# An adaLN block with multi-query attention: a lead in another order, and one scale on another engine

## The chip, the cores and the metric

The kernel runs on one core of a Trainium2 chip. A core has five engines that run their own instruction queues in order: TensorE (PE in the profile; its weight loads are PEld), VectorE (DVE), ScalarE (ACT), GpSimd (POOL) and SyncE (SP, which here only issues DMAs). An instruction starts when the one before it on its engine has been issued and every semaphore that it needs is set. The metric is the device time of one execution in microseconds.

## The reference

The inputs are one batch of S = 2048 rows of width D = 512, one conditioning vector c, and weights. There are H = 32 query heads of size 16 that share one K head and one V head, and F = 1792.

```python
mod = (_silu(c) @ w_mod).reshape(c.shape[0], 6, 1, -1)
sa, ca, ga, sb, cb, gb = (mod[:, 0], mod[:, 1], mod[:, 2], mod[:, 3], mod[:, 4], mod[:, 5])
h = _layernorm(x, axis=-1) * (1 + ca) + sa
x = x + ga * _A_ref(h, A_wq, A_wk, A_wv, A_wo)      # softmax attention, 32 heads, one K and one V
h = _layernorm(x, axis=-1) * (1 + cb) + sb
x = x + gb * _B_ref(h, B_w_gate, B_w_up, B_w_down)  # ((h Wg) * (h Wu)) Wd
```

## The kernel before

The rows are cut into 4 blocks of 512. A unit is one block of queries with 4 of the 32 heads, so there are 32 units; a block's x lies in two groups of 256 rows (`xts[2b]` and `xts[2b+1]`, of two tiles each). Matmuls that need precision run as two f16 halves, high and low, so an operand such as h or wq is first split: a high half, and the rest as a low half.

Softmax subtracts a row maximum. It is computed ahead by the max pass: for each unit PE multiplies q by all keys (L569), DVE reduces each 128x512 result (L573), and the maxima are put into the q tile `sst[u]` as two more rows. While a unit's scores, exponentials and PV products run (`attend`, L620, L622, L631), the max pass of the next unit runs between them. Side work (q projections of later units, weight preparation, the output projection and the gated FFN, all at L484 on PE) fills the gaps.

Before the first unit can attend, everything up to its maxima has to be there. That is the lead. A straight part first loads x, w_mod and wq, computes the modulation, the norm of block 0 and its h, and the first K and q projections. A loop of 30 steps follows (`LEAD`), which for each step n emits, in this order: what was posted before, the max pass, the relus left over, `first[n]`, some matmuls of the first q projection of block 0 (`Q_BURSTS`, steps 26 to 29), and one of the pieces that compute the rest of the modulation (from step 23 on). The max pass does two of its own steps in lead steps 0, 2, ... 12, none in the odd ones up to 13, and one in each from 14 to 29. The first unit has 24 of them: 16 with two plain reduces each (L573; the first 8 over the keys of block 0, the other 8 over block 1), and for blocks 2 and 3 a "diff" matmul pair (keys of block 3 minus those of block 2, for which `kng` holds the negated keys of block 2) whose relu ACT takes (L576) and a combined add and maximum on DVE (L578), 16 in all. The second unit's start at lead step 24.

The dictionary `first` is the order that is written out by hand. Engines are in-order and the schedule is manual, so an entry's place fixes where its instructions stand in each engine's queue. The entries are:

- `ln_stats(i)`: bn_stats and bn_aggr of group i on DVE (L238, L240). `ln_rstd(b)`: the reciprocal deviation of block b on POOL, eight small instructions (L200 to L205, L312, L313). `ln_norm(b, ...)`: four tiles normalised, here two on DVE and two on ACT (L251, L249).
- `ln_tr(b)`: per 128 columns four PE transposes into one PSUM bank (L257) and an ACT evacuation to `hf(b, k)` with the modulation (L260).
- `k_part(b)`, `q_part(u, p)`: eight PE matmuls (L267) and an ACT copy (L269). `combine(key, sel)`: one f32 matmul (two passes, L274) that adds the partial sums and lays out the rows. `k_evac(b)`, `q_evac(u, p)`: the f16 halves of K or q, a high half on ACT (L288) and the rest on DVE (L289). Unit u has two q tiles p = 0, 1; both first units are projected in the lead from block 0's h.
- `v_mm(b)`: eight small PE matmuls (L302), and an ACT copy (L305) posted for the next step.
- `h_halves(b, ks)`: the halves of h of block b on POOL. For block 0 the tile is first scaled in place by `fwd[:, 0:1]` (L422), so a q projection from block 0's unscaled h has to stand ahead of it. Then L424 and L425.
- `wq_squares(ks)`: squares with row sums on ACT (L402). `wq_sum`: their sum over partitions on PE, a DVE reduce, and a power and a scale on POOL (L406 to L410). `wq_scales`: a DVE reciprocal (L413) and two small POOL instructions. `wq_halves(ks)`: the high half on ACT (L420), a scale and the low half on POOL (L422, L425).
- `last_rows()`: the load of the other half of w_mod (3 MB) into the space of x's blocks 0 to 2 (L439). `ev_scales`: constants for the output.

PSUM has eight banks of 128x512 f32, handed out in turn from a queue (`ps_hold`, `ps_give`, `ps_mx`, `ps_sc`): a matmul that is given a bank waits until the one that used it before has been read. `posts` are closures emitted at the start of the next step.

Two pieces of the straight part matter as well: the scales for K, q and h that are computed from four maxima (L359 to L373), and what follows them, in the order `combine(0)`, `combine((0, 0))`, `ln_norm(1)` on DVE, `k_evac(0)`, `q_evac(0, 0)`, `q_part(0, 1)`, `ln_norm(1)` on ACT, `ln_stats(4)`, `ln_stats(5)`, `ln_rstd(2)`.

Of the kernel before, what the change touches and what calls it, by code (L numbers as in the profile page):

```python
# [54 lines left out]
def adaln_mqa_glu_kernel(ctx: ExitStack, tc: tile.TileContext, x_in, wq_in, wk_in, wv_in, wo_in,  # L55
# [175 lines left out]
    def ln_stats(i):  # L231
        if i % 2 == 0:
            stats[i // 2] = (work.tile([128, 4, 2], F32, name="st"), work.tile([128, 4], F32, name="ry0"),
                             work.tile([128, 8], F32, name="nb0"))
        st = stats[i // 2][0]
        bs = [work.tile([128, 6], F32, name="bs", bufs=4) for _ in range(2)]
        for t in range(2):
            nc.vector.bn_stats(bs[t], xts[i][t])  # L238
        for t in range(2):
            nc.vector.bn_aggr(st[:, 2 * (i % 2) + t, :], bs[t])  # L240

    def ln_norm(b, engines):
        st, y, nb = stats[b]
        for j, eng in enumerate(engines):
            if eng is None:
                continue
            xt = xts[2 * b + j // 2][j % 2]
            if eng is nc.scalar:
                nc.scalar.activation(xt, xt, AF.Identity, bias=nb[:, 4 + j:5 + j], scale=y[:, j:j + 1])  # L249
            else:  # L250
                eng.tensor_scalar(xt, xt, st[:, j, 0:1], y[:, j:j + 1], op0=OP.subtract, op1=OP.mult)  # L251
# [20 lines left out]
    def combine(key, sel):  # L272
        p = pks[key] = ps_hold("pk")
        nc.tensor.matmul(p, sel.rearrange("p a r -> p (a r)"), parts[key], start=True, stop=True)  # L274

    def k_part(b):
        partial(b, wkv, b)

    def q_part(u, p):
        partial((u, p), wqs[:, :, 64 * u + 32 * p:64 * u + 32 * p + 32], 0)  # L280

    def q_evac(u, p):
        split_rows(sst[u][:, p, :], pks[u, p], qsc, sck[:, 3:4], 0.0)
        ps_give(pks[u, p])
# [6 lines left out]
    def k_evac(b):  # L291
        cs = slice(b * BT, (b + 1) * BT)
        sc = sckb if b else sck
        split_rows(kst[:, cs], pks[b], sc[:, 0:1], sc[:, 2:3], rows[:, 2:3])
        if b == NB - 2:
            nc.gpsimd.tensor_scalar(kng, kst[:, cs], -1.0, 0.0, op0=OP.mult, op1=OP.add)
        ps_give(pks[b])

    def v_mm(b):
        p = ps_hold("pvt", (128, 4, 16))  # L300
        for i in range(4):
            nc.tensor.matmul(p[:, i, :], parts[b][:, i * 128:(i + 1) * 128], lane[:, 16:32], start=True, stop=True)  # L302

        def out():
            nc.scalar.activation(vst[:, 4 * b:4 * b + 4, 0:16], p, AF.Copy, scale=inv[:, 0:1] if b else 1.0)  # L305
            ps_give(p)
        posts.append(out)

    def ln_rstd(b):
        st, y, nb = stats[b]  # L310
        rstd_into(y, st[:, :, 1], 4)
        nc.gpsimd.tensor_tensor(nb[:, 0:4], st[:, :, 0], y, op=OP.mult)  # L312
        nc.gpsimd.tensor_scalar(nb[:, 4:8], nb[:, 0:4], -1.0, 0.0, op0=OP.mult, op1=OP.add)  # L313
# [53 lines left out]
    qsc = sck[:, 1:2]  # L367
    nc.vector.reciprocal(sck[:, 0:1], kb[:, 6:7])
    nc.vector.tensor_tensor(sck[:, 2:3], rows[:, 0:1], sck[:, 0:1], op=OP.mult)
    nc.gpsimd.tensor_scalar(inv[:, 0:1], kb[:, 4:5], 22.64 * 1.001 * 2.0 ** -15, 2.0 ** -45, op0=OP.mult, op1=OP.max)  # L370
    nc.vector.reciprocal(fwd[:, 0:1], inv[:, 0:1])
    nc.vector.tensor_scalar(hsb, modT[0][:, :, 0:64:32], fwd[:, 0:1], None, op0=OP.mult)
    nc.gpsimd.tensor_scalar(sckb, sck, inv[:, 0:1], 0.0, op0=OP.mult, op1=OP.add)  # L373
    combine(0, selk)
    combine((0, 0), selq)
    ln_norm(1, (nc.vector, None, nc.vector, None))
    k_evac(0)
    q_evac(0, 0)
    q_part(0, 1)
# [57 lines left out]
    def last_rows():  # L437
        wmb = big.tile([128, KC, 1536], F32, name="wmB", tag="wu")
        nc.sync.dma_start(wmb, wm_v[:, :, 1536:3072])  # L439
        wmB.append(wmb)  # L440

    wmB = []
    KA, KB = (0, 1), (2, 3)
    ln_stats(4)
    ln_stats(5)
    ln_rstd(2)
    SA, VE = nc.scalar, nc.vector
    first = {0: lambda: (combine((0, 1), selq), ln_tr(1)),
             1: lambda: (q_evac(0, 1), v_mm(0), ln_stats(6)),
             2: lambda: (k_part(1), ln_norm(2, (VE, SA, VE, SA)), ln_stats(7), ln_rstd(3)),  # L450
             3: lambda: combine(1, selk), 4: lambda: (k_evac(1), ln_tr(2)),
             5: lambda: (last_rows(), ln_norm(3, (VE, SA, VE, SA))),
             6: lambda: (k_part(2), v_mm(1)), 7: lambda: combine(2, selk),
             8: lambda: (k_evac(2), ln_tr(3)), 9: lambda: (q_part(1, 0), v_mm(2)),
             10: lambda: (k_part(3), combine((1, 0), selq), h_halves(3, KA)),
             11: lambda: (q_evac(1, 0), combine(3, selk)), 12: lambda: (k_evac(3), h_halves(3, KB), q_part(1, 1), wq_squares(KA)),
             13: lambda: (v_mm(3), combine((1, 1), selq), wq_squares(KB)), 14: lambda: (q_evac(1, 1), wq_sum()),
             15: lambda: h_halves(0, KA), 16: wq_scales, 17: lambda: h_halves(0, KB), 19: lambda: wq_halves(KA), 20: ev_scales, 21: lambda: wq_halves(KB),
             23: lambda: h_halves(1, KA), 24: lambda: h_halves(1, KB)}
    later_h = deque((2, k) for k in range(KC))  # L460

    TERMS = ((0, 0), (1, 0), (0, 1))
# [816 lines left out]
```

## Time and profile before

| | |
|---|---|
| median of 3 runs | 1686.23 us (1686.07 to 1686.28) |
| profiled execution | 1688.73 us |
| its span, first to last instruction | 1686.7 us |
| mean granted TensorE clock | 0.997 |
| PE busy | 1661.1 us, 98% |
| DVE busy | 1389.7 us, 82% |
| ACT busy | 1217.1 us, 72% |
| POOL busy | 517.2 us, 31% |
| first scores of attention (L620) | 80.56 us from the span's start |

The profile is of one execution under the hardware profiler, so its own time stands beside its span. An engine's busy time is a sum over the whole span and hides stages: PE is busy 98% because it carries attention and the FFN for 1600 us, while the lead is its first 80 us. Where the prediction shows rows in order of time, a row gives start, length, engine, line and operation, the tile written and those read, how many instructions were merged into the row, and in brackets the idle time of the engine just before and what ended it. Matmul lengths include the pipeline, so the distance between starts tells more of a matmul's cost than its length.

### The profile page before, as it was taken

The numbers are of one execution on the slowest core, as the hardware profiler recorded it, in microseconds if no ns is written. First come the engines' busy times: TensorE is split into PE (matmuls) and PEld (weight loads), VectorE is DVE, ScalarE is ACT, GpSimd is POOL, SyncE is SP. The second block draws the span as 40 slices with busy tenths as digits, with TensorE's granted clock in tenths as the row PEclk, the third lists the DMA queues.
The fourth block names the chain that finished last, engine by engine and source line by source line (L and its number), as shares of the span: only waits on it lengthen the run. The fifth ranks groups of instructions, "written<-read, shape, count | busy, mean of one in ns | idle before, by whom it ended". The sixth has DMA issues, their size and how long they took to land.

```text
span 1686.7 us, 33353 instructions
## 1 busy us (share of the span) xinstructions
PE 1661.1 (98%) x12749; PEld 538.2 (32%) x12749; DVE 1389.7 (82%) x2364; ACT 1217.1 (72%) x2288; POOL 517.2 (31%) x691
## 2 busy tenths in 40 slices
PE   8999999999999999999999999999999999999999
PEld 3333333222223333333333333333333333334444
DVE  7899999999999999999989999999998999703110
ACT  5688888888887878777777777777777777772010
POOL 3754364626676750110040110101022111112230
PEclk9899999999999999999999999999999999999999
DMA  6112122212322210001100000000010000001000
GB/s 228 74 49 87 50 90 63 86 37 61 90 66 60 77 30 10 17 9 29 35 11 16 14 17 10 16 10 17 24 32 12 22 15 7 12 5 47 15 1 25
DMA packets 48556, 66.33 MB, mean 39 GB/s; under 512 B 14726, under 2 KB 29194, under 8 KB 48396
## 3 DMA queue, kind: packets, MB, share of 16 engines
q1 hardware_dynamic: 46812, 63.87, 12.5%
q8 instruction: 100, 1.64, 0.4%
q14 instruction: 60, 0.49, 0.1%
q10 hardware_dynamic: 1584, 0.33, 0.1%
HBM read 51.05 MB, written 8.65 MB: 35 GB/s over the span
## 4 chain that ended last, share of the span: by engine, by line
PE 88%; DVE 8%; ACT 2%; POOL 1%; issue 1%; DMA 0%; ACTq 0%; POOLq 0%
PE side L484 50%; PE pv L631 27%; DVE mpart L573 7%; PE sc L620 5%; PE mx L569 3%; ACT P L622 1%; PE misc L159 1%; PE mx L764 1%; PE part L267 0%; PE pk L274 0%; PE mxt L597 0%; POOL h L425 0%; POOL wq L425 0%; DVE bs L238 0%; ACT kwb L260 0%
## 5 line engine op out<-in xcount | busy, mean ns | idle before, releaser
L573 DVE TENSOR_REDUCE mpart<-mx 128x1 f32<-128x512 f32 x2016 | 1266.9, 684 | 95.3 <-PE mx L569 91.4
L622 ACT ACTIVATE P<-sc 128x512 f32<-128x512 f32 x2048 | 1091.6, 599 | 265.6 <-PE sc L620 221.7
L620 PE MATMUL sc<-sst,kst 50*128 50x512 f16 x2048 | 660.9, 379 | 0.8 <-DVE mpart L573 0.6
L569 PE MATMUL mx<-kst,sst 48*128 48x512 f16 x2032 | 619.7, 377 | 6.9 <-DVE mpart L573 4.2
L631 PE MATMUL pv<-P,vst 128*32 128x512 f32 x4096 | 545.3, 605 | 1.2
L484 PE MATMUL side<-h2T,wg 64*128 64x512 f16 (+1 forms) x1168 | 284.6, 378 | 0.1
L484 PE MATMUL side<-h2T,wu 64*128 64x512 f16 (+1 forms) x1166 | 282.9, 378 | 0.0
L484 PE MATMUL side<-wd,glu 64*128 64x512 f16 (+1 forms) x1008 | 234.0, 378 | 0.0
L817 POOL TENSOR_SCALAR glu<-gf 128x512 f16<-128x512 f32 x56 | 34.8, 621 | 617.7 <-DVE gf L816 539.1
L620 PEld LDWEIGHTS <-kst 50*128 50x128 f16 x2048 | 175.2, 94 | 129.5 <-issue 109.5
L569 PEld LDWEIGHTS <-sst 48*128 48x128 f16 x2064 | 185.5, 94 | 56.6 <-issue 33.5
L484 PEld LDWEIGHTS <-wg 64*128 64x128 f16 (+1 forms) x1168 | 100.7, 95 | 202.8 <-ACT P L622 94.9
L484 PEld LDWEIGHTS <-wu 64*128 64x128 f16 (+1 forms) x1166 | 100.8, 95 | 199.9 <-ACT P L622 92.2
L631 PEld LDWEIGHTS pv<-P,vst 128*32 128x32 f32 x4096 | 80.8, 108 | 218.7 <-issue 202.7
L484 PEld LDWEIGHTS <-glu 64*128 64x128 f16 (+1 forms) x1008 | 89.1, 95 | 162.9 <-ACT P L622 62.9
L816 DVE TENSOR_TENSOR gf<-side,g 128x512 f32<-128x512 f32 x56 | 38.4, 685 | 115.8 <-PE side L484 82.5
L484 PE MATMUL side<-h,wq 64*128 64x512 f16 (+1 forms) x349 | 92.8, 376 | 0.9 <-POOL wq L425 0.9
L811 ACT ACTIVATE g<-side 128x512 f32<-128x512 f32 x56 | 33.2, 593 | 81.5 <-PE side L484 81.5
L484 PE MATMUL side<-wo,och 64*128 64x512 f16 (+1 forms) x336 | 79.3, 378 | 0.0
L818 POOL TENSOR_TENSOR glu<-gf,glu 128x512 f16<-128x512 f32 x56 | 65.0, 1161 | 4.7
L200 POOL TENSOR_SCALAR rv<-st 128x1 f32<-128x1 f32 (+1 forms) x20 | 4.6, 229 | 165.0 <-DVE st L724 142.4
L665 POOL TENSOR_TENSOR oc<-oc,rr 128x512 f32<-128x512 f32 x15 | 19.1, 1273 | 109.2 <-DMA sst<-qd 94.8
(223 smaller groups left out, 815.1 us busy)
## 6 DMA issues: line engine op xcount, KB each, us to landing
wsl<-in_B_w_gate_dram SPq DMA_DIRECT2D x32, 224.0 KB
wsl<-in_B_w_up_dram SPq DMA_DIRECT2D x32, 224.0 KB
wsl<-in_B_w_down_dram SPq DMA_DIRECT2D x28, 256.0 KB
sst<-qd SPq DMA_DIRECT2D x180, 32.0 KB
oc<-ev SPq DMA_DIRECT2D x128, 32.0 KB
rr<-ri SPq DMA_DIRECT2D x16, 256.0 KB
xl<-in_A_x_dram SPq DMA_DIRECT2D x16, 256.0 KB
qd<-q SPq DMA_DIRECT2D x15, 256.0 KB
```

What stands on the lines that cost most here:

```text
L159: nc.tensor.matmul(pwarm, warm[:, 0:128], warm, start=True, stop=True)
L484: return nc.tensor.matmul(self.p, left[64 * r0:64 * r1], right[64 * r0:64 * r1], start=start, stop=self.ended())
L569: nc.tensor.matmul(m, s[64 * a:64 * a + 48, p, t * 128:(t + 1) * 128], w[64 * a:64 * a + 48, :], start=(i == 0), stop=(i == len(keys) - 1))
L573: nc.vector.tensor_reduce(part, m, axis=AX.X, op=OP.max)
L620: nc.tensor.matmul(t, kst[64 * a:64 * a + 50, kt * 128:(kt + 1) * 128], s[64 * a:64 * a + 50, p, :], start=True, stop=True)
L622: ex = nc.scalar.activation(ptl[u, kt, p, a], t, AF.Exp)
L631: nc.tensor.matmul(pvb[u][32 * j:32 * j + 32, :], vst[:, kt, :], ptl[u, kt, p, a], start=(kt == 0), stop=(kt == KT - 1))
L665: eng.tensor_tensor(o, o, st["r"], op=OP.mult)
L811: nc.scalar.activation(st["g", f], p, AF.Copy, scale=2.0 ** -45)
L816: nc.vector.tensor_tensor(gf, p, st["g", f], op=OP.mult)
L817: nc.gpsimd.tensor_scalar(st["glu"][:, 0, f, :], gf, 1.0, 0.0, op0=OP.mult, op1=OP.add)
L818: nc.gpsimd.tensor_tensor(st["glu"][:, 1, f, :], gf, st["glu"][:, 0, f, :], op=OP.subtract)
```

## The change

It moves calls within the lead and moves one instruction from POOL to DVE; every other instruction is the same. The scale `inv[:, 0:1]` (L370) is computed on DVE. `ln_stats(4)` moves ahead of `k_evac(0)`. In `first`, both q projections of the second unit go from steps 9 and 12 to step 1 and their evacuations from 11 and 14 to 4 and 6; the norms of the third block go from step 2 to 1 and those of the fourth from 5 to 4, with the transposes behind them (4 to 3, 8 to 6); the squares of wq go from 12 and 13 to 4 and 5, its sum from 14 to 7, its scales from 16 to 8, its halves from 19 and 21 to 9 and 10; the halves of h of block 0 go from 15 and 17 to 2 and 5, those of block 3 from 10 and 12 to 12 and 13, those of block 1 from 23 and 24 to 15 and 17.

```diff
-    nc.gpsimd.tensor_scalar(inv[:, 0:1], kb[:, 4:5], 22.64 * 1.001 * 2.0 ** -15, 2.0 ** -45, op0=OP.mult, op1=OP.max)
+    nc.vector.tensor_scalar(inv[:, 0:1], kb[:, 4:5], 22.64 * 1.001 * 2.0 ** -15, 2.0 ** -45, op0=OP.mult, op1=OP.max)
     nc.vector.reciprocal(fwd[:, 0:1], inv[:, 0:1])
     nc.vector.tensor_scalar(hsb, modT[0][:, :, 0:64:32], fwd[:, 0:1], None, op0=OP.mult)
     nc.gpsimd.tensor_scalar(sckb, sck, inv[:, 0:1], 0.0, op0=OP.mult, op1=OP.add)
     combine(0, selk)
     combine((0, 0), selq)
     ln_norm(1, (nc.vector, None, nc.vector, None))
+    ln_stats(4)
     k_evac(0)
     q_evac(0, 0)
     q_part(0, 1)
...
-    ln_stats(4)
     ln_stats(5)
     ln_rstd(2)
     SA, VE = nc.scalar, nc.vector
     first = {0: lambda: (combine((0, 1), selq), ln_tr(1)),
-             1: lambda: (q_evac(0, 1), v_mm(0), ln_stats(6)),
-             2: lambda: (k_part(1), ln_norm(2, (VE, SA, VE, SA)), ln_stats(7), ln_rstd(3)),
-             3: lambda: combine(1, selk), 4: lambda: (k_evac(1), ln_tr(2)),
-             5: lambda: (last_rows(), ln_norm(3, (VE, SA, VE, SA))),
-             6: lambda: (k_part(2), v_mm(1)), 7: lambda: combine(2, selk),
-             8: lambda: (k_evac(2), ln_tr(3)), 9: lambda: (q_part(1, 0), v_mm(2)),
-             10: lambda: (k_part(3), combine((1, 0), selq), h_halves(3, KA)),
-             11: lambda: (q_evac(1, 0), combine(3, selk)), 12: lambda: (k_evac(3), h_halves(3, KB), q_part(1, 1), wq_squares(KA)),
-             13: lambda: (v_mm(3), combine((1, 1), selq), wq_squares(KB)), 14: lambda: (q_evac(1, 1), wq_sum()),
-             15: lambda: h_halves(0, KA), 16: wq_scales, 17: lambda: h_halves(0, KB), 19: lambda: wq_halves(KA), 20: ev_scales, 21: lambda: wq_halves(KB),
-             23: lambda: h_halves(1, KA), 24: lambda: h_halves(1, KB)}
+             1: lambda: (q_evac(0, 1), v_mm(0), ln_norm(2, (VE, SA, VE, SA)), ln_stats(6), ln_stats(7),
+                         q_part(1, 0), q_part(1, 1)),
+             2: lambda: (k_part(1), h_halves(0, (0,)), ln_rstd(3)),
+             3: lambda: (combine((1, 0), selq), combine(1, selk), ln_tr(2)),
+             4: lambda: (k_evac(1), q_evac(1, 0), ln_norm(3, (VE, SA, VE, SA)), wq_squares(KA)),
+             5: lambda: (combine((1, 1), selq), k_part(2), v_mm(1), h_halves(0, (1, 2, 3)), last_rows(),
+                         wq_squares(KB)),
+             6: lambda: (q_evac(1, 1), combine(2, selk), ln_tr(3)),
+             7: wq_sum, 8: lambda: (k_evac(2), v_mm(2), wq_scales()),
+             9: lambda: (k_part(3), wq_halves(KA)), 10: lambda: (combine(3, selk), v_mm(3), wq_halves(KB)),
+             12: lambda: (k_evac(3), h_halves(3, KA)), 13: lambda: h_halves(3, KB),
+             15: lambda: h_halves(1, KA), 17: lambda: h_halves(1, KB), 20: ev_scales}
```

## The prediction

> **What bounds the kernel now.** The change touches only the lead, so I first read the busy time of the engines over stretches that I cut myself: the lead in three, then ten us of attention.
>
> ```profile
> 30.10:61.05 30.95, 25.92 (x147) 11.39 (x146) 25.82 (x48) 20.05 (x37) 11.03 (x21) 0.92 0.27 103
> 61.05:72.10 11.05, 9.80 (x57) 4.59 (x53) 10.31 (x37) 9.72 (x18) 10.31 (x15) 0.76 0.01 1
> 72.10:81.05 8.95, 7.72 (x48) 2.20 (x49) 7.77 (x15) 1.38 (x5) 8.45 (x13) 1.00 0.13 40
> ...
> 90.00:100.00 10.00, 9.97 (x84) 3.14 (x80) 9.92 (x17) 8.25 (x17) 9.66 (x11) 1.00 0.31 107
> ```
>
> The columns are the length, the busy time (and instructions) of PE, PE's loads, DVE, ACT and POOL, then the granted clock and two of DMA. In attention PE and DVE are both full: nothing is to be won there. In the lead DVE has holes: 30.95 - 25.82 = 5.13 us, 11.05 - 10.31 = 0.74, and 8.95 - 7.77 = 1.18, together 7.05. The change leaves DVE's work in these stretches the same within 0.1 us, so the lead can end 7.05 us sooner at most, and the question is which of the holes close and which open. The waits of DVE, the first two rows from the first stretch and the others from the rest (total us, times, longest), say who ends them:
>
> ```profile
> DVE mpart L573 <- PE mx L569: 3.8, 3, 1.9
> DVE sst L289 <- ACT hi L288: 1.7, 3, 0.9
> ```
>
> ```profile
> DVE mpart L573 <- PE mx L569: 1.2, 3, 0.6
> DVE rel L578 <- ACT rel L576: 0.6, 1, 0.6
> ```
>
> (The second row has a third wait, 0.34 us, just ahead of the stretch.) The early holes come out of PE's queue, where set-up matmuls stand ahead of the max matmuls, and out of ACT's. The later ones come from the halves. POOL in order of time (in brackets the idle time before, and what ended it): a block's reciprocal deviations take from 37.01 to 40.07, then it idles until K of block 2 at 47.86, starts halves, idles once more, and from 60 us on never stops.
>
> ```profile
> 37.01 0.24 POOL L200 TENSOR_SCALAR rv<-st 128x4 f32<-128x4 f32 x1 [6.82 <-DVE st L240]
> ...
> 39.87 0.20 POOL L313 TENSOR_SCALAR nb<-nb 128x4 f32<-128x4 f32 x1
> 47.86 0.63 POOL L296 TENSOR_SCALAR kwb<-kst 128x512 f16<-128x512 f16 x1 [7.80 <-DVE kst L289]
> ...
> 60.01 0.55 POOL L409 TENSOR_TENSOR wqt<-wqt,phalf 128x1 f32<-128x1 f32 x1 [4.21 <-DVE wqt L408]
> ...
> 61.00 0.69 POOL L422 TENSOR_SCALAR kwb<-kwb,fwd 128x512 f32<-128x512 f32 x1
> ...
> 79.03 1.16 POOL L425 TENSOR_TENSOR wq<-wqst,wq 128x512 f16<-128x512 f32 x1
> ```
>
> The last half of wq ends at 80.2 us, and the q matmuls of the lead's end (L484), which read it, stand on PE ahead of DVE's max matmuls: that is the 1.2 us row. ACT's own halves of wq stand between its relus: the 0.6 us row.
>
> **Durations.** The chain of waits gives them (start, length, what); a row that covers several gives the time from the first's start to the last's end.
>
> ```profile
> 24.50 0.54 PE mx L569 x4
> 25.04 1.05 PE pk L274 x2
> 26.10 0.45 PE sc L257 x4
> ...
> 32.24 2.37 DVE mpart L573 x4
> 34.61 0.91 DVE xbig L251 x2
> 35.52 1.20 DVE bs L238 x2
> 36.72 0.22 DVE st L240 x2
> ...
> 40.38 1.00 PE part L267 x8
> 41.38 0.99 PE pvt L302 x8
> 42.38 1.69 PE pk L274 x2
> 44.06 0.97 PE mx L569 x4
> ...
> 55.33 0.72 ACT wqj L402 x2
> ```
>
> On DVE four max reduces are 2.4 us, a pair of norms 0.9, a call of ln_stats 1.4. On PE four max matmuls are 0.55, a combine 1.05, a projection 1.0, v_mm 1.0, a block's 16 transposes 4 x 0.45 = 1.8. On ACT a square with its read is 0.72. On POOL a scaled half is 0.7 + 0.7 + 1.16 = 2.6 by the rows at 61.00 and 79.03, an unscaled half or one of wq 1.9. More, of ACT and then of DVE in order of time:
>
> ```profile
> 24.31 1.51 ACT L249 ACTIVATE xbig<-xbig,nb,ry 128x512 f32<-128x512 f32 x2
> 26.57 2.89 ACT L260 ACTIVATE kwb<-sc,hsb 128x512 f32<-128x512 f32 x4 [0.75 <-PE sc L257]
> 29.37 0.68 ACT L288 ACTIVATE hi<-pk,sck 128x512 f16<-128x512 f32 x1
> ```
>
> ```profile
> 21.47 0.16 DVE L371 RECIPROCAL fwd<-inv 128x1 f32<-128x1 f32 x1 [1.62 <-POOL inv L370]
> ...
> 25.59 1.25 DVE L238 BATCH_NORM_STATS2 bs<-xbig 128x6 f32<-128x512 f32 x2
> ...
> 27.25 2.48 DVE L573 TENSOR_REDUCE mpart<-mx 128x1 f32<-128x512 f32 x4
> 30.08 0.75 DVE L289 SCALAR_TENSOR_TENSOR sst<-pk,sck,hi 128x512 f16<-128x512 f32 x1 [0.34 <-ACT hi L288]
> ...
> 61.04 0.68 DVE L578 CUSTOM_DVE_ANT_0 rel<-mx,rel 128x512 f32<-128x512 f32 x1
> ```
>
> **The K scale on DVE, and ln_stats(4) sooner: 0.** L370 on DVE costs about what L371 costs, 0.16 to 0.2 us, and DVE's wait of 1.62 us goes: DVE is 1.4 us ahead. ln_stats(4), 1.4 us, fills just that ahead of k_evac(0), whose ACT half comes no sooner. After the two evacuations ln_stats(5), the second call before the reduces, ends at 25.6 (its row at 25.59 moves up by one call), and step 0's reduces run from 25.85, not 27.25, to 28.3. But DVE's next instruction, the evacuation at 30.08, waits for ACT's hi at 29.37, behind ACT's norms and the evacuation of block 1's transposes; neither moves. So it starts at 30.08 as before, with 1.8 us of idle ahead of it in place of 0.34. From there both kernels have the same DVE work to do. Bounds: a loss of 0.2 (the added instruction, if ACT were not the later one) to a gain of 0.3.
>
> **First stretch, walked by hand.** *Step 1.* Evacuation, norms of block 2, ln_stats(6) and (7) keep DVE to 34.5 (0.7 + 0.9 + 2.8). The deviations that these norms read take POOL 3.0 us after ln_stats(5) at 25.6: ready. PE, done with block 1's transposes at 26.05 + 1.8 = 27.85, does v_mm(0), both q projections of the second unit (to 30.9), step 2's max matmuls, block 1's K projection (32.4) and, in step 3, two combines (34.4). *Steps 2 to 4.* DVE reduces to 36.9. On PE, block 2's transposes now stand ahead of step 4's max matmuls and take the PSUM banks that these reduces free one by one, so step 4 starts no sooner than 36.9: a hole of **0.5**. Reduces to 39.75; ACT evacuates the transposes from 35.0 to 37.85 and has both hi at 39.2, in time; two evacuations and block 3's norms take DVE to 41.95. *Steps 5 and 6.* A combine, a projection, v_mm and max matmuls keep PE to 41.15, ahead of DVE's reduces, 41.95 to 44.35. ACT goes through norms (40.6), two squares (42.1), block 2's K part (42.7), two squares (44.1), the v copy, and only then the hi of the second unit's other half, at 45.0: a hole of **0.7**. *Steps 7 and 8.* The K combine waited on PE for that K part, so it ends at 43.75, block 3's transposes at 45.75, the sum of squares at 46.0, and step 8's max matmuls follow: holes of **0.65**. Reduces to 48.9, K of block 2, then the reciprocal for wq. POOL has its input at 47.2 (one scaled half 30.9 to 33.5, deviations 34.6 to 37.6, three halves to 45.5, root and scale of the sum). *Steps 9 to 14.* Block 3's projection, K part and combine and v_mm keep PE to 51.9; reduces run 49.75 to 52.15 and, after **0.15**, to 54.7.
>
> Holes: 0.5 + 0.7 + 0.65 + 0.15 = 2.0 in place of 5.13. The cover is thin: on ACT there is hardly a gap from 35 to 53.5, so whatever is added there is added here.
>
> **Second stretch.** ACT's halves of wq stand in steps 9 and 10, under reduces, and not between relus: 0.1 in place of 0.74. **Third stretch.** POOL's work is all done ahead: halves of wq by 58.3, of block 3 by 65.6, of block 1 by 73; the burst matmuls, from step 26 near 70 us, would wait again if wq came 12 us later than that. What stays is PE's queue in step 26 (three q matmuls, 0.82 by the row below, and a row of the modulation ahead of step 27): 0.4 in place of 1.18. The load of wmB stays in step 5, past no other SP issue, and waits for block 2's transposes, done at 36.75.
>
> ```profile
> 74.28 0.82 PE L484 MATMUL side<-h,wq 128*128 128x512 f16 x3
> ...
> 80.56 0.39 PE L620 MATMUL sc<-sst,kst 50*128 50x512 f16 x1
> ```
>
> **Sum.** 7.05 - (2.0 + 0.1 + 0.4) = 4.55 us, and from 81 us on the same order runs on full engines, so it reaches the end. The profiled execution took 1688.73 us for a span of 1686.7 (2.0 around it, 2.5 above the median); it would take 1684.2. The median becomes 1686.23 - 4.6 = **1681.6**; for this case alone 3.5 to 6 us less, 1680.2 to 1682.7. A difference under 0.2%, 3.4 us, can't be told from none here.
>
> **Rivals.** *The clock.* The granted clock halves twice in the lead:
>
> ```profile
> 42.00:44.00 2.00, 2.00 (x8) 0.51 (x7) 1.26 (x3) 0.44 (x2) 0.00 (x0) 0.61 1.01 424
> ...
> 56.00:58.00 2.00, 0.93 (x4) 0.10 (x2) 1.53 (x3) 1.91 (x6) 0.00 (x0) 1.00 0.00 0
> 60.00:66.00 6.00, 6.00 (x30) 3.90 (x29) 6.00 (x20) 5.56 (x11) 5.47 (x8) 0.50 0.00 0
> ```
>
> The first cost PE 0.65 us on a combine (1.69 beside 1.05) and 0.43 on max matmuls (0.97 beside 0.54), with the transposes behind about 1.6; the second, after PE had idled half of 56 to 58, nothing, for DVE stayed full. In the new order PE idles most from 52.5 to 55.5, so I expect the halved clock again under the combined reduces, at no cost. The Trainium skill (TensorE: Matmul & The Clock Gate, Part 1) says that the clock halves after an idle window of about 3.4 us; the last two rows agree, the first, where PE was merely thin, does not show it. If it halves between 41 and 47 instead, where PE waits 1.6 us for the K part: 1.6 us back, 1683.2. Chance 0.12.
>
> *ACT is the bound.* My walk gives ACT 0.7 for an evacuation; four took 2.89, and whole instructions some 0.07 more than their spacing. Over the 24 instructions from 35 to 53.5 that is 1.8 us: 1683.4. Against it, 26.57 to 29.37 is 2.8 for four. Chance 0.08.
>
> *DVE and POOL in each other's way.* The norms of blocks 2 and 3 read and write SBUF alone, and now run beside POOL's halves; before, POOL was near idle in all of them (39.87: 0.2 us). If each pair waits for one two-input instruction of POOL, 2 x 1.16 = 2.3 us return: 1683.9. Chance 0.06. The Trainium skill (Advanced Engine Details and Errata, VectorE Performance Modes) says that DVE's two-port modes and POOL's instructions block each other; no run here shows it.
>
> *Slower.* The clock stays halved from 34 us to the end of the lead, as the thin stretches follow each other. PE's 14.6 us of work from 34.4 to 52.5, at 1.6 times (1.69 by 1.05), takes 8.8 more, 3.5 of it in gaps; the 6.5 us that PE sets at the lead's end 3.9 more: 9.2 - 4.6 = 4.6 slower, 1690.8. It decides from 7.7 us of such work on. Against it: the longest halved stretch before is little over the 6 us of the row above. Chance 0.06.
>
> **From these to the numbers.** Forecast 0.68: faster 0.68, same 0.12 + 0.08 + 0.06 = 0.26, slower 0.06. The range reaches from 1679.9 (0.6 us of holes in the first stretch, and 0.3 from the start) to 1683.9 and leaves out the last rival and the forecast's edges.
>
> **What would show it.** Right: the evacuation of the first unit's second half still at about 30.1; holes of some 2 us from there to the first combined reduce, at about 58; POOL idle before the lead's end; no wait of PE for wq; attention's first scores (L620) near 76 in place of 80.6. Wrong: DVE holes behind PE from 41 to 50 with the clock at 0.5 (first rival), ACT full and late (second), norms over 0.55 us (third).

## The result and the profile after

The changed kernel takes 1683.28 us (median of 11 runs, 1682.07 to 1683.67), the kernel before 1686.69 us (median of 11, 1686.07 to 1690.9). The ratio over the rounds is 0.9974, 95% interval 0.9966 to 0.9983: 4.4 us less, between 2.9 and 5.7; by the medians it is 3.4 us. The times are not spread evenly. Of the eleven of the change, four lie between 1682.07 and 1682.76 and seven between 1683.18 and 1683.67 (below: the lower and the upper group); of the eleven before, nine lie between 1686.07 and 1687.0, one at 1688.27 and one at 1690.9. The profiled execution of the change took 1682.67 us with a span of 1680.6, 6.1 us under the first profile of before, and attention's first scores stand at 74.38 us, 6.18 sooner. It belongs to the lower group of its kernel, while the first profile of before, 1688.73 us, lies above most executions of its own. So the two profiles are further apart than the kernels are; the second profile of before, below, shows why.

In the changed file the lines from L408 on are one or more further down, so the max reduce is L574, the max matmul L570 and the scores L621. The stretches of the prediction, cut in the new profile at the same events (the evacuation of the first unit's second q half, the first combined reduce, the last one, attention's first reduce):

```profile
28.99:57.06 28.07, 22.87 (x140) 10.87 (x134) 27.54 (x49) 21.38 (x41) 20.91 (x33) 0.94 0.29 113
57.06:67.13 10.07, 9.81 (x58) 3.24 (x54) 10.04 (x35) 7.09 (x14) 9.65 (x12) 0.83 0.01 2
67.13:75.17 8.04, 7.67 (x48) 2.35 (x50) 7.65 (x15) 1.67 (x5) 5.65 (x9) 1.00 0.05 18
```

DVE (third busy time) idles 28.07 - 27.54 = 0.53 us in the first stretch, 0.03 in the second and 0.39 in the third, where it idled 5.13, 0.74 and 1.18. But its busy time in the first stretch has grown from 25.82 to 27.54, although its instructions are the same but for a reciprocal. DVE in order of time says where:

```profile
19.17 0.15 DVE L370 TENSOR_SCALAR inv<-kb 128x1 f32<-128x1 f32 x1
19.35 0.16 DVE L371 RECIPROCAL fwd<-inv 128x1 f32<-128x1 f32 x1
...
28.99 0.75 DVE L289 SCALAR_TENSOR_TENSOR sst<-pk,sck,hi 128x512 f16<-128x512 f32 x1 [1.51 <-ACT hi L288]
29.66 1.75 DVE L251 TENSOR_SCALAR xbig<-xbig,st,ry 128x512 f32<-128x512 f32 x2
31.34 1.27 DVE L238 BATCH_NORM_STATS2 bs<-P 128x6 f32<-128x512 f32 x2
...
37.04 2.48 DVE L574 TENSOR_REDUCE mpart<-mx 128x1 f32<-128x512 f32 x4 [0.47 <-PE mx L570]
...
40.76 2.16 DVE L251 TENSOR_SCALAR P<-P,st,ry 128x512 f32<-128x512 f32 x2
...
45.24 0.73 DVE L289 SCALAR_TENSOR_TENSOR sst<-pk,sck,hi 128x512 f16<-128x512 f32 x1
45.90 0.14 DVE L409 TENSOR_REDUCE wqt<-sc 128x1 f32<-128x4 f32 x1
...
71.51 11.01 DVE L574 TENSOR_REDUCE mpart<-mx 128x1 f32<-128x512 f32 x18 [0.39 <-PE mx L570]
```

The wait of L371 for POOL is gone, and comes back as 1.51 us ahead of the evacuation at 28.99. Of the walk's holes the one of 0.47 at step 4 is there. The norms (L251) took 0.91 us from their start to the next instruction's in the kernel before; now it is 31.34 - 29.66 = 1.68 and 42.85 - 40.76 = 2.09, together 1.95 us more. The waits for ACT's hi at step 6 and for the sum of squares at step 7 do not show, since the longer norms cover them. POOL in order of time:

```profile
29.68 0.70 POOL L423 TENSOR_SCALAR kwb<-kwb,fwd 128x512 f32<-128x512 f32 x1 [1.75 <-ACT xbig L249]
...
40.73 0.62 POOL L425 TENSOR_SCALAR h<-kwb 128x512 f16<-128x512 f32 x1
41.44 1.20 POOL L426 TENSOR_TENSOR h<-kwb,h 128x512 f16<-128x512 f32 x1
42.62 0.86 POOL L423 TENSOR_SCALAR kwb<-kwb,fwd 128x512 f32<-128x512 f32 x1
...
71.38 1.16 POOL L426 TENSOR_TENSOR h<-kwb,h 128x512 f16<-128x512 f32 x1
```

POOL's scaled halves of block 0 run from 29.68 and again from 37.32, and so beside both pairs of norms. POOL's large work is done at 72.5, before the lead is, and no q matmul waits for it.

### The profile page after: what moved, and what is told of

The parts are those of the page before. It is cut to its first block, busy times and chain, and to the rows that moved or that the text cites. A ratio compares the mean times of both kernels' runs of the same rounds, so it can differ in the third digit from the quotient of the medians.

```text
span 1680.6 us, 33352 instructions
## 1 busy us (share of the span) xinstructions
PE 1656.3 (99%) x12749; PEld 535.4 (32%) x12749; DVE 1390.0 (83%) x2365; ACT 1216.1 (72%) x2288; POOL 518.1 (31%) x690
## 4 chain that ended last, share of the span: by engine, by line
PE 87%; DVE 9%; ACT 2%; DMA 1%; issue 0%; ACTq 0%; DVEq 0%
PE side L485 50%; PE pv L632 27%; DVE mpart L574 8%; PE sc L621 5%; PE mx L570 3%; ACT P L623 2%; PE mx L765 1%; DMA xbig<-in_A_x_dram 1%; PE mxt L598 0%; DVE bs L238 0%; PE sc L570 0%; PE pk L274 0%; DMA wkv<-in_A_wv_dram 0%; DVE rel L579 0%; PE part L267 0%
## 5 line engine op out<-in xcount | busy, mean ns | idle before, releaser
L574 DVE TENSOR_REDUCE mpart<-mx 128x1 f32<-128x512 f32 x2016 | 1266.1, 683 | 91.6 <-PE mx L570 88.3
L621 PE MATMUL sc<-sst,kst 50*128 50x512 f16 x2048 | 661.0, 379 | 1.0 <-DVE mpart L574 0.8
L570 PE MATMUL mx<-kst,sst 48*128 48x512 f16 x2032 | 617.3, 377 | 6.5 <-DVE mpart L574 3.8
L621 PEld LDWEIGHTS <-kst 50*128 50x128 f16 x2048 | 175.2, 94 | 129.4 <-issue 109.6
L570 PEld LDWEIGHTS <-sst 48*128 48x128 f16 x2064 | 183.9, 94 | 58.7 <-issue 37.4
```

Source lines behind the costliest of these rows:

```text
L570: nc.tensor.matmul(m, s[64 * a:64 * a + 48, p, t * 128:(t + 1) * 128], w[64 * a:64 * a + 48, :], start=(i == 0), stop=(i == len(keys) - 1))
L574: nc.vector.tensor_reduce(part, m, axis=AX.X, op=OP.max)
L621: nc.tensor.matmul(t, kst[64 * a:64 * a + 50, kt * 128:(kt + 1) * 128], s[64 * a:64 * a + 50, p, :], start=True, stop=True)
```

## The experiments

**The kernel before, profiled again.** Unchanged.

> The kernel before, unchanged, profiled a second time, to see which of the differences between the two profiles belong to a single execution. Theory: the start of attention's first scores (80.56 us in the first profile) moves by up to 1.2 us, because the modulation's row copy (L331) stood 1.25 us later in the first profile of before than in the one of after, in code that is the same in both; and the halved clock at 42 to 46 us, with its hole of about 1.4 us ahead of step 8's reduces, is not in every execution. Rival: start and clock dip are where they were within 0.2 us, and the whole 6.1 us between the two spans is the change.

It took 1686.07 us with a span of 1684.0, and the scores stand at 77.93, 2.63 us sooner than in the first profile. The same three stretches, two rows of the clock (the third column from the end), and DVE's waits at steps 8 and 10, in this profile and then in the first one:

```profile
29.06:58.45 29.39, 25.27 (x147) 12.01 (x146) 25.84 (x48) 20.21 (x37) 11.03 (x21) 0.93 0.29 108
58.45:69.46 11.01, 10.14 (x57) 4.80 (x53) 10.29 (x37) 9.59 (x18) 10.27 (x15) 0.73 0.01 1
69.46:78.39 8.93, 7.69 (x48) 2.17 (x49) 7.76 (x14) 1.35 (x5) 8.43 (x13) 1.00 0.10 31
```

```profile
36.00:38.00 2.00, 2.00 (x11) 1.50 (x10) 2.00 (x4) 1.85 (x4) 1.67 (x4) 0.71 0.02 4
...
42.00:44.00 2.00, 2.00 (x16) 1.33 (x16) 1.58 (x4) 1.30 (x2) 0.00 (x0) 1.00 1.01 424
```

```profile
42.67 2.48 DVE L573 TENSOR_REDUCE mpart<-mx 128x1 f32<-128x512 f32 x4 [0.42 <-PE mx L569]
...
47.09 2.48 DVE L573 TENSOR_REDUCE mpart<-mx 128x1 f32<-128x512 f32 x4 [1.28 <-PE mx L569]
```

```profile
44.63 2.48 DVE L573 TENSOR_REDUCE mpart<-mx 128x1 f32<-128x512 f32 x4 [1.37 <-PE mx L569]
...
49.70 2.48 DVE L573 TENSOR_REDUCE mpart<-mx 128x1 f32<-128x512 f32 x4 [1.92 <-PE mx L569]
```

The first stretch has 29.39 - 25.84 = 3.55 us of holes, not 5.13. The two at steps 8 and 10 are 0.42 and 1.28 where the first profile had 1.37 and 1.92: 1.59 us less, with the clock at 1.00 from 42 to 46 and not at 0.61 and 0.53. The clock did halve here too, but from 33.7 to 37.2 us (0.71 in the row of 36 to 38), where DVE was full and had no hole. The other 1.0 us is the start: the evacuation stands at 29.06, not at 30.08, in code that both share. The theory holds: 2.6 of the 6.2 us between the first two profiles belong to one execution of before. This profile and the one of the change begin the first stretch together (29.06, 28.99) and both had the clock at 1.00 from 40 to 47: from there to attention's first reduce it is 49.33 and 46.18 us, so the change is worth 3.15 us there.

**The straight part undone.**

```diff
-    nc.vector.tensor_scalar(inv[:, 0:1], kb[:, 4:5], ...
+    nc.gpsimd.tensor_scalar(inv[:, 0:1], kb[:, 4:5], ...
-    ln_stats(4)
     k_evac(0)
     q_evac(0, 0)
...
+    ln_stats(4)
     ln_stats(5)
```

> The change with its straight part undone: the K scale on GpSimd again and ln_stats(4) behind q_evac(0, 0). Theory of the prediction: both are worth nothing, as VectorE waits for ScalarE's high half at the end of step 0 anyway; that wait falls from 1.5 to about 0.3 us, everything after it starts at the same time, and the run is within 0.3 us of the change, some 3.4 to 4.6 us under before. Rival: the lead is 0.5 to 1.4 us longer, since the VectorE time saved ahead of that wait reaches the end.

1683.77 us (1681.70 to 1683.96), ratio to before 0.9976 [0.9966, 0.9986]: within 0.5 us of the change. DVE in order of time:

```profile
21.24 0.17 DVE L371 RECIPROCAL fwd<-inv 128x1 f32<-128x1 f32 x1 [1.60 <-POOL inv L370]
...
29.86 0.75 DVE L289 SCALAR_TENSOR_TENSOR sst<-pk,sck,hi 128x512 f16<-128x512 f32 x1 [0.34 <-ACT hi L288]
30.53 0.99 DVE L251 TENSOR_SCALAR xbig<-xbig,st,ry 128x512 f32<-128x512 f32 x2
```

The 1.60 us are back at L371 and gone from the evacuation, as the theory has it. From L359 to the evacuation it is 11.6 us here and 11.13 in the change, but 11.40 and 11.51 in two of the runs below that have the new straight part, so up to there a part of up to 0.5 us stays open; 1.4 us it is not. At the end nothing is left of it: this profile has the halved clock at 42 to 46 us (0.54 and 0.61), as has the second profile of the change below, and from L359 to attention's first scores it is 57.41 us here and 57.62 there.

**Halves of h of block 0 late.**

```diff
-             2: lambda: (k_part(1), h_halves(0, (0,)), ln_rstd(3)),
+             2: lambda: (k_part(1), ln_rstd(3)),
-             5: lambda: (combine((1, 1), selq), k_part(2), v_mm(1), h_halves(0, (1, 2, 3)), last_rows(),
+             5: lambda: (combine((1, 1), selq), k_part(2), v_mm(1), last_rows(),
-             12: lambda: (k_evac(3), h_halves(3, KA)), ...
+             11: lambda: h_halves(0), 12: lambda: (k_evac(3), h_halves(3, KA)), ...
```

> The change with all halves of h of block 0 moved to step 11, behind wq's, so that GpSimd is idle beside the norms of blocks 2 and 3. Theory: the two pairs of norms on VectorE, 1.75 and 2.16 us in the change, go back to 0.99 us each because no long GpSimd instruction runs beside them; and the 1.95 us that VectorE wins there come back as holes (for ScalarE's high half near 43.6 us and for the sum of squares), so the time stays within 0.6 us of the change. First rival: the stretched norms were on the path, and the run is 1.5 to 2 us faster than the change. Second rival: the norms stay at 1.7 to 2.2 us, so GpSimd was not the cause.

1682.10 us (1681.42 to 1683.68), ratio 0.9971 [0.9961, 0.9982]. DVE in order of time:

```profile
29.79 0.99 DVE L251 TENSOR_SCALAR xbig<-xbig,st,ry 128x512 f32<-128x512 f32 x2
...
40.13 1.00 DVE L251 TENSOR_SCALAR P<-P,st,ry 128x512 f32<-128x512 f32 x2
...
43.68 0.75 DVE L289 SCALAR_TENSOR_TENSOR sst<-pk,sck,hi 128x512 f16<-128x512 f32 x1 [0.16 <-ACT hi L288]
44.81 0.16 DVE L409 TENSOR_REDUCE wqt<-sc 128x1 f32<-128x4 f32 x1 [0.38 <-PE sc L407]
45.13 2.48 DVE L574 TENSOR_REDUCE mpart<-mx 128x1 f32<-128x512 f32 x4 [0.15 <-PE mx L570]
```

With POOL idle beside them the norms are back at 0.99 and 1.00: POOL's halves stretched them. The holes that they had covered open, 0.16 + 0.38 + 0.15 = 0.69. From the evacuation to the first scores it is 73.55 - 29.12 = 44.43 us, in the change 74.38 - 28.99 = 45.39. Both had the clock at 1.00 up to 52 us. So 0.96 of the 1.95 us had reached the end (0.69 if counted from L359, 55.83 and 56.52 us), more than the theory's 0.6 and less than the first rival's 1.5.

**The first unit's q evacuated in step 0.**

```diff
-    first = {0: lambda: (combine((0, 1), selq), ln_tr(1)),
-             1: lambda: (q_evac(0, 1), v_mm(0), ...
+    first = {0: lambda: (combine((0, 1), selq), q_evac(0, 1), ln_tr(1)),
+             1: lambda: (v_mm(0), ...
```

> The change with the evacuation of the first unit's second q half emitted in step 0 ahead of the transposes of block 1, and not in step 1. Theory: in the change VectorE is the bound from 29 to 74 us, with one hole of 0.47 us, so the hole of 1.5 us ahead of that evacuation is worth itself: it closes to under 0.3 us and the run is 1.0 to 1.5 us faster than the change (5 to 6 us under before). Rival: ScalarE and TensorE are the real bound behind it; the hole opens again ahead of step 4 or step 6 and the time stays within 0.4 us of the change.

1682.77 us (1681.89 to 1683.38), ratio 0.9970 [0.9961, 0.9979]: 0.5 us under the change by the medians, so the 1.0 to 1.5 us of the theory did not come, and the rival's 0.4 is nearly met. The hole of 1.5 us is closed, the one at step 4 doubles, and another opens at step 7, with the clock at 0.50:

```profile
27.84 0.74 DVE L289 SCALAR_TENSOR_TENSOR sst<-pk,sck,hi 128x512 f16<-128x512 f32 x1
...
35.63 2.48 DVE L574 TENSOR_REDUCE mpart<-mx 128x1 f32<-128x512 f32 x4 [0.97 <-PE mx L570]
...
46.04 0.16 DVE L409 TENSOR_REDUCE wqt<-sc 128x1 f32<-128x4 f32 x1 [1.43 <-PE sc L407]
```

As this profile has a halved clock and the first one of the change has not, those two do not tell what q alone is worth. The second profile of the change, below, has it at nearly the same place: from L359 to the first scores it is 56.60 us here and 57.62 there, 1.0 us less. So with the clock the same q alone is worth about 1 us of the 1.5 in one pair of profiles, and 0.5 by the medians.

**PE kept busy.** In the change, with extra matmuls whose results are overwritten:

```diff
+    def busy(p, n):
+        for _ in range(n):
+            nc.tensor.matmul(p, sst[2][:, 0, 0:128], sst[2][:, 0, :], start=True, stop=True)
...
-             3: lambda: (combine((1, 0), selq), combine(1, selk), ln_tr(2)),
+             3: lambda: (combine((1, 0), selq), combine(1, selk), ln_tr(2, n=5)),
...
-             6: lambda: (q_evac(1, 1), combine(2, selk), ln_tr(3)),
+             6: lambda: (q_evac(1, 1), combine(2, selk, 5), ln_tr(3)),
```

> The change with five extra 128x512 f16 matmuls on zeros ahead of the transposes of block 2 and five ahead of the K combine of block 2, in the bank that these overwrite, so in PE time that is idle in the change (1.3 us at 33.5 and 1.4 us at 40.8). Theory: the runs of the change fall into two groups 1.1 us apart (1682.1 to 1682.8, 1683.2 to 1683.7) because the granted clock halves between 40 and 47 us in some executions and not in others; with PE kept busy it stays at 1.00 there, the upper group is gone, and the median falls by 0.5 to 1.0 us to 1682.2 to 1682.8. First rival: the clock is as before, two groups and a median within 0.3 us of 1683.3. Second rival: the extra matmuls delay what stands behind them and the run is 0.5 us or more slower.

1682.67 us, and all six runs lie between 1682.36 and 1682.92; ratio 0.9969 [0.9957, 0.9980]. This is what the theory said: the upper group is gone, and the median is 0.6 us lower. The clock of the profiled run is at 1.00 from 14 to 54 us. PE in order of time has the fill in its gaps, ahead of a combine that starts no later than in the change (42.20):

```profile
40.94 1.24 PE L255 MATMUL pk<-sst 128*128 128x512 f16 x5
42.22 1.13 PE L280 MATMUL pk<-part,selk 128*128 128x512 f32 x2
```

**The change again.** Unchanged, for a second profile.

> The change itself, unchanged, on the same chip as the run above and with a second profile. Theory: times again in two groups, near 1682.5 and 1683.5, with a median between 1682.4 and 1683.6; if its profiled execution is of the upper group, the granted clock is near 0.5 somewhere between 40 and 47 us, and VectorE has a hole of 1 to 1.5 us ahead of the sum of squares that the first profile of the change did not have. Rival: the upper group has the clock at 1.00 there and loses its time elsewhere.

1683.16 us: 1682.17, 1682.27, 1682.75, and 1683.57, 1683.80, 1684.10. The profiled one is 1683.57, and it has what the theory asked for, the clock and the hole:

```profile
42.00:44.00 2.00, 1.99 (x6) 1.25 (x7) 2.00 (x4) 1.97 (x6) 1.89 (x3) 0.69 1.02 427
44.00:46.00 2.00, 2.00 (x12) 2.00 (x11) 1.77 (x3) 1.67 (x4) 1.16 (x1) 0.50 0.93 381
```

```profile
46.71 0.16 DVE L409 TENSOR_REDUCE wqt<-sc 128x1 f32<-128x4 f32 x1 [0.95 <-PE sc L407]
47.03 2.48 DVE L574 TENSOR_REDUCE mpart<-mx 128x1 f32<-128x512 f32 x4 [0.16 <-PE mx L570]
```

Under the halved clock block 3's 16 transposes on PE take 3.37 us (from 43.18), in the first profile of the change 2.13 (from 43.16). DVE's two holes behind them, 0.95 + 0.16 = 1.1 us, are the distance of the groups. Over both sets of runs of the change 10 of 17 are in the upper one; with PE kept busy none of six is. Besides this one, the profile of the run with the straight part undone (1683.77 us, of its kernel's upper group) has the same clock and a hole of 0.98 at the same place.

**The norms alone, the halves alone.** Both on the new straight part; the norms with their transposes and K projections, or else q, squares, sum, scales and halves, stand as in the change, the rest at the steps of before. The changed entries of the first, then of the second:

```diff
+             1: lambda: (q_evac(0, 1), v_mm(0), ln_norm(2, (VE, SA, VE, SA)), ln_stats(6), ln_stats(7)),
+             2: lambda: (k_part(1), ln_rstd(3)), 3: lambda: (combine(1, selk), ln_tr(2)),
+             4: lambda: (k_evac(1), ln_norm(3, (VE, SA, VE, SA))),
+             5: lambda: (k_part(2), v_mm(1), last_rows()), 6: lambda: (combine(2, selk), ln_tr(3)),
+             8: lambda: (k_evac(2), v_mm(2)), 9: lambda: q_part(1, 0),
```

```diff
+             1: lambda: (q_evac(0, 1), v_mm(0), ln_stats(6), q_part(1, 0), q_part(1, 1)),
+             2: lambda: (k_part(1), ln_norm(2, (VE, SA, VE, SA)), ln_stats(7), h_halves(0, (0,)), ln_rstd(3)),
+             3: lambda: (combine((1, 0), selq), combine(1, selk)),
+             4: lambda: (k_evac(1), q_evac(1, 0), ln_tr(2), wq_squares(KA)),
+             5: lambda: (combine((1, 1), selq), last_rows(), ln_norm(3, (VE, SA, VE, SA)), h_halves(0, (1, 2, 3)),
+                         wq_squares(KB)),
+             6: lambda: (q_evac(1, 1), k_part(2), v_mm(1)), 7: lambda: (combine(2, selk), wq_sum()),
+             8: lambda: (k_evac(2), ln_tr(3), wq_scales()), 9: lambda: (v_mm(2), wq_halves(KA)),
+             10: lambda: (k_part(3), wq_halves(KB)), 11: lambda: combine(3, selk),
...
+             13: lambda: (v_mm(3), h_halves(3, KB)),
```

> The straight part and the norms, transposes and K projections in the new order; q of the second unit, squares, sum, scales and all halves at the steps of before. Theory: this closes the VectorE holes behind TensorE at steps 4 to 8 (1.7 us in the second profile of before), leaves the three of 0.51, 0.47 and 0.86 us at steps 11 to 14, and leaves those of the lead's end (1.8 us), since GpSimd still goes without a break from the sum of squares to the lead's end: 1.2 to 1.9 us under before. Rival: this part carries all of it, 3 us or more.

> The straight part, q of the second unit, squares, sum, scales and halves in the new order; norms, transposes and K projections at the steps of before. Theory: the lead's end no longer waits for GpSimd (1.2 us) nor the relus for ScalarE's halves of wq (0.6 us), and the holes at steps 11 to 14 go (1.8 us), but those behind TensorE at steps 4 to 8 stay or grow, as two projections and two combines more stand there, and one pair of norms is stretched by GpSimd: 1.5 to 2.8 us under before. First rival: 3.4 us or more, this part carries all. Second rival: under 1 us, as the early steps give back what the end wins.

Norms alone: 1683.85 us (1683.50 to 1684.44 and one run at 1687.80), 2.9 under the median of before on that chip, 1686.76; ratio 0.9981 [0.9971, 0.9990], or 3.2 us. Halves alone: 1685.96 (1684.24 to 1686.66), 0.8 under; ratio 0.9989 [0.9980, 0.9998], or 1.9 us. The norms give more than the theory's 1.2 to 1.9 us. For the halves the two measures part: by the medians they fall under 1 us, which was the second rival, by the ratio they lie within the theory's 1.5 to 2.8. That the norms carry most is so by the medians; the intervals of the two ratios overlap. DVE in order of time, norms alone first:

```profile
48.50 0.75 DVE L289 SCALAR_TENSOR_TENSOR sst<-pk,sck,hi 128x512 f16<-128x512 f32 x1 [0.27 <-ACT hi L288]
...
54.61 0.75 DVE L289 SCALAR_TENSOR_TENSOR sst<-pk,sck,hi 128x512 f16<-128x512 f32 x1 [0.86 <-ACT hi L288]
...
75.02 7.62 DVE L572 TENSOR_REDUCE mpart<-mx 128x1 f32<-128x512 f32 x12 [0.58 <-PE mx L568]
```

```profile
46.25 0.16 DVE L409 TENSOR_REDUCE wqt<-sc 128x1 f32<-128x4 f32 x1 [1.98 <-PE sc L407]
46.79 2.48 DVE L573 TENSOR_REDUCE mpart<-mx 128x1 f32<-128x512 f32 x4 [0.37 <-PE mx L569]
...
50.45 2.48 DVE L573 TENSOR_REDUCE mpart<-mx 128x1 f32<-128x512 f32 x4 [0.45 <-PE mx L569]
54.25 2.48 DVE L573 TENSOR_REDUCE mpart<-mx 128x1 f32<-128x512 f32 x4 [1.32 <-PE mx L569]
```

Norms alone leave the waits for POOL at the end (0.58 of DVE, where a q matmul on PE waits 0.45 us for POOL's half of wq) and of q's evacuation (0.86), and close those behind PE at steps 8 and 10. Halves alone close the end, and DVE now waits 4.1 us for PE between 44 and 55, as every transpose and projection of blocks 2 and 3 stands in front of the max matmuls, behind two projections and two combines more. The wait of 1.98 us has the clock at 0.55 (44 to 46 us), so a part of the 4.1 us may belong to this one execution.

**A version that beats both.** First with the three losses taken together: q in step 0, norms and halves apart, squares behind block 2's K part.

```diff
+    first = {0: lambda: (combine((0, 1), selq), q_evac(0, 1), ln_tr(1)),
+             1: lambda: (v_mm(0), ln_norm(2, (VE, SA, VE, SA)), ln_stats(6), ln_stats(7),
+                         q_part(1, 0), q_part(1, 1)),
+             2: lambda: (k_part(1), ln_rstd(3), h_halves(0)),
+             3: lambda: (combine((1, 0), selq), combine(1, selk), ln_tr(2), ln_norm(3, (VE, None, VE, None))),
+             4: lambda: (k_evac(1), q_evac(1, 0), ln_norm(3, (None, SA, None, SA))),
+             5: lambda: (combine((1, 1), selq), k_part(2), v_mm(1), last_rows()),
+             6: lambda: (q_evac(1, 1), combine(2, selk), wq_squares(KA), ln_tr(3)),
+             8: lambda: (k_evac(2), wq_squares(KB), v_mm(2)),
+             9: lambda: (k_part(3), wq_sum()), 10: lambda: (combine(3, selk), v_mm(3), wq_scales(), wq_halves(KA)),
+             11: lambda: wq_halves(KB), 12: lambda: (k_evac(3), h_halves(3, KA)), 13: lambda: h_halves(3, KB),
```

> The change, and in addition: q of the first unit evacuated in step 0 (as in the run before that had this alone); block 3's reciprocal deviations ahead of all halves of block 0 on GpSimd, and its norms on VectorE in step 3, where VectorE waits for step 4's matmuls, so that norms and halves hardly meet; squares of wq behind the K part of block 2 on ScalarE. Theory: the hole of 1.5 us ahead of the first evacuation, the 0.5 to 1.0 us at step 4 and most of the 1.95 us of stretched norms go, and the K combine of block 2 comes 1.4 us sooner, with VectorE the bound to the lead's end: 1.8 to 3 us faster than the change, 1680.3 to 1681.5. Rival: ScalarE is the bound from 35 us on, and the time is within 0.6 us of the run with q sooner (1682.8).

1681.73 us (1681.65 to 1682.52), ratio 0.9967 [0.9955, 0.9980]: 1.5 us under the change, a little less than the 1.8 to 3 expected. DVE in order of time: norms at full speed, and two holes from ACT's squares and halves of wq.

```profile
35.12 1.00 DVE L251 TENSOR_SCALAR P<-P,st,ry 128x512 f32<-128x512 f32 x2 [0.22 <-POOL ry L205]
...
47.48 0.16 DVE L409 TENSOR_REDUCE wqt<-sc 128x1 f32<-128x4 f32 x1 [0.90 <-PE sc L407]
...
53.84 0.75 DVE L289 SCALAR_TENSOR_TENSOR kst<-pk,sckb,hi 128x512 f16<-128x512 f32 x1 [1.11 <-ACT hi L288]
```

Then with those two moved out of the way:

```diff
-             8: lambda: (k_evac(2), wq_squares(KB), v_mm(2)),
-             9: lambda: (k_part(3), wq_sum()), 10: lambda: (combine(3, selk), v_mm(3), wq_scales(), wq_halves(KA)),
-             11: lambda: wq_halves(KB), 12: lambda: (k_evac(3), h_halves(3, KA)), 13: lambda: h_halves(3, KB),
+             8: lambda: (k_evac(2), v_mm(2)), 9: lambda: (k_part(3), wq_squares(KB)),
+             10: lambda: (combine(3, selk), v_mm(3), wq_sum()),
+             12: lambda: (wq_scales(), k_evac(3), wq_halves(KA + KB), h_halves(3, KA)), 13: lambda: h_halves(3, KB),
```

> The run without meetings of norms and halves (1681.73), with the second two squares of wq behind block 3's K part, their sum in step 10 behind the max matmuls, and the scale's reciprocal and all four halves of wq in step 12, the halves behind ScalarE's high half of K of block 3. Theory: the three holes of VectorE that the run before still had there (0.41 us stays, 0.90 + 0.16 ahead of the sum, 1.11 ahead of K of block 3) shrink by 1.5 us, of which about 0.4 comes back because the first relus now wait for ScalarE's halves of wq: 0.8 to 1.4 us faster, 1680.3 to 1680.9. Rival: the relus wait longer than that, and the time is within 0.4 us of 1681.7.

1679.64 us, all six runs between 1679.23 and 1679.94; ratio to before 0.9949 [0.9937, 0.9962], 3.5 us under the change on the same chip. Against the run before it is 2.1 us, more than the theory's 0.8 to 1.4: the holes of 0.90 and 1.11 are gone, those of 0.41 and 0.16 stay, and the 0.4 that was to come back at the relus did not:

```profile
48.23 0.16 DVE L409 TENSOR_REDUCE wqt<-sc 128x1 f32<-128x4 f32 x1
...
51.02 0.73 DVE L289 SCALAR_TENSOR_TENSOR kst<-pk,sckb,hi 128x512 f16<-128x512 f32 x1
...
54.21 0.69 DVE L578 CUSTOM_DVE_ANT_0 rel<-mx,rel 128x512 f32<-128x512 f32 x1
```

## Why the prediction was right, and where it was off

**The time.** 1681.6 was forecast and 1683.28 measured; 4.6 us of gain against 3.4 by the medians and 4.4 [2.9, 5.7] by the ratio. The time lies inside the range up to 1683.9, but outside the 1680.2 to 1682.7 that the prediction gave its own case: the range holds it only because it was stretched for the first three rivals. The gain of 3.4 us by the medians also stands right at the size that the prediction said can't be told from none, though the interval of the ratio lies wholly below 1. Of the prediction's three signs of being wrong, two were seen: holes of DVE behind PE with the clock at 0.5 (in one of two profiles), and norms over 0.55 us (in both). So the way in which the lead is shortened was right, and the gain was forecast too large. That the range reached far enough, for two rivals with chances of 0.12 and 0.06 that both came in part, is more luck than reckoning. Two terms were mis-sized: the baseline of 7.05 us of holes, and the price of the norms.

**The straight part: 0.** As reasoned: the time won ahead of the evacuation came back as 1.51 us of waiting (1.8 forecast), and undoing it moved the time by no more than 0.5 us.

**First stretch.** The walk said 2.0 us lost. It was 0.53 of holes and 1.95 of stretched norms, together 2.5. (The stretch as a whole came out only 0.25 us longer than 30.95 - 5.13 + 2.0 = 27.82, as DVE's busy time grew by 1.72.) The hole of 0.5 at step 4 was 0.47; those of 0.7 and 0.65 lay under the norms and showed up, at 0.16 and 0.53, once the norms were short again. The walk's step that failed is the price of a pair of norms, 0.9 us: it was taken from rows where POOL was idle. That was the third rival, given 0.06: its mechanism is shown by moving POOL's halves away, its price of 2.3 us was near the 1.95 measured, and 0.7 to 1.0 of it reached the end. The page's rule that it named (the Trainium skill, Advanced Engine Details and Errata, VectorE Performance Modes) agrees with these runs: a norm takes 0.54 us beside an idle POOL and up to 1.37 beside its halves.

**The baseline.** The holes of before were read off one execution. 1.59 us of the 5.13 in its first stretch belonged to a halved clock from 42 to 46 us that its second profile did not have. The prediction knew the price (1.6) and used it for a rival of the new kernel, but did not ask how often before paid it: it took the 4.55 us, with these 1.59, off a median of executions that for the most part do not have them. The 66 executions of before in all these runs lie in three groups, 43 up to 1687.4, 10 near 1688.4, where the first profile's time is, and 13 near 1691.2. The same dip is in the new kernel too: 10 of 17 runs lie 1.1 us higher, and the one of them with a profile has it. So by the times the first rival (0.12, at 1683.2) happens in more than half of the executions, and the median of 1683.28 is in its group; its price was 1.1 us and not 1.6. With the dip in neither profile or in both, the gain from L359 to the first scores is 60.37 - 56.52 = 3.85 and 62.10 - 57.62 = 4.48 us; the medians' 3.4 sets a kernel mostly without it against one mostly with it.

Two things on the clock stay open. The group of before near 1691 has no profile; its mean granted clock, 0.993 to 0.995 where it is recorded, is the lowest (0.995 to 0.998 in the other two), and none of the 17 runs of the change is more than 1 us above its median, but whether the change has anything to do with that is not shown. And the prediction read the halving at 60 us as agreeing with the idle window of about 3.4 us that it cites, but PE's longest gap there was 1.42 us (58.35), and it was busy 1.98 of the 3.4 us from 56.0 to 59.4, so no trace here shows such a window.

The forecast that the clock would halve under the combined reduces at no cost was right: from 54 to 60 us it is at 0.50, and the reduces at 57.06, 57.66 and 58.27 still start 0.61 us apart.

**Second and third stretch.** 0.03 for 0.1, and 0.39 for 0.4, at the place forecast. POOL was done at 72.5 (73), the first combined reduce came 28.07 us after the evacuation (27.9), and the gain of 6.18 us at the scores is 6.1 at the end, so nothing behind the lead took any of it back. Of ACT as the bound (second rival) there is no sign in the change: its rows at 37.5 to 45 us are under 0.9 us from the walk's, relative to the evacuation. The slower rival did not come about: the longest halved stretch in the two profiles of the change is about 7 us.

**What carries it.** The sum took the second and third stretch, the end of the lead, for 0.64 + 0.78 = 1.4 of 4.55 us. Apart, the norms gave 2.9 us and the halves 0.8 by the medians (3.2 and 1.9 by the ratios): halves sooner close the end, but pay for it in PE's queue unless the norms and transposes move too.

## What to carry to other kernels

Before holes of one profile are added up, take a second profile of the same kernel, and see where the profiled time lies among the others: here 2.6 us of the 6.2 between two profiles was one execution's. A walk through in-order queues with prices from rows predicted each stretch within 0.5 us, but a price holds only beside the same neighbours: an engine that was idle when the price was taken belongs to it. And work that is moved out of the critical engine's way pays most where it does not land beside work that slows it: parting norms and halves and moving the evacuation, squares and scales to where DVE was busy gave as much again as the change, 1679.6 us.

## What the runs showed of the hardware that was not expected

- A DVE tensor_scalar over 128x512 f32, SBUF to SBUF, takes 0.54 us beside an idle POOL; beside POOL's scaled halves the four of the change's norms took 0.83 to 1.37 (its two pairs 1.68 and 2.09 for 0.91). POOL's scale beside the second pair takes 0.86 for 0.70. bn_stats beside the same POOL instructions (31.34: 1.27 for two) and reduces out of PSUM are as before.
- The granted clock halves in one execution and not in the next at about the same place (42 to 46 us). That alone parts the times by 1.1 us in the new kernel, and made 1.59 us of holes in a profile of the old. The stretch ahead of it is not idle: from 36 to 42 us PE is busy 4.60 of 6 us in the first profile of before and 4.64 in the second of the change, with no gap over 1.4 us. Nor does this share decide it: with block 0's halves late PE is busy 4.63 us there, and the clock stays at 1.00.
- Ten filling matmuls in 2.7 us of PE's gaps (PE busy 5.92 of these 6 us) went with the clock at 1.00 there in the one profile taken, and with all six times in the lower group, against 7 of 17 without them. One of the two profiles without them has the clock at 1.00 as well, so it is the times that speak for the fill.
- The first 18 us, the same code in all, varied by 0.9 us: the copy at L359 stood between 17.56 and 18.46.
